# Transposing u on VectorE and through DRAM for the last groups of every batch, with other DMA queues, buffers and load order

## The chip, the cores and the metric

The kernel runs on one core of one Trainium2 chip. The metric is the device time of one execution in microseconds. A core has TensorE (PE, matmuls into PSUM), VectorE (DVE), ScalarE (ACT), GpSimd (POOL) and SyncE (SP), each with an in-order instruction stream of its own. DMAs are issued here from SP's and GpSimd's queues and move their bytes on 16 DMA engines that all queues share.

## The reference

Eight batches of a sequence of 3136 rows by 256 columns. First a filter in the frequency domain along the sequence, then a low-rank mix along the sequence, then a two-layer network along the columns with a residual:

```python
X = np.fft.rfft(x, axis=1)
y = np.fft.irfft(X * F, n=3136, axis=1)            # F: 1569 x 256, complex
u = y + (y.transpose(0, 2, 1) @ U @ V).transpose(0, 2, 1)   # rank 32
out = u + np.maximum(u @ w_ch1, 0.0) @ w_ch2       # 256 -> 1024 -> 256
```

## The kernel before

The Fourier transform of length 3136 is done as 49 x 64. A batch goes through five steps. `f1` (L241; L269 for batches 0 and 1) multiplies the tiles x of the input by the matrix ws, copies the result on ScalarE into a tile asb and stores it to the DRAM tensors ct1 and ct0 from SP. `mid` (L319) loads it back as a2, multiplies by m (matmul pz, L384), by the filter on DVE (uv, L392, L396, L397), transforms back (matmul pe, L345), copies on ScalarE to e and stores to the DRAM tensors ct2 (three parts, L364, from SP). `load_e2` (L412) loads the rows of ct2 into the rows of one tile eb, 256 KB per DMA: for each part one DMA for the half h = 0 (first 32 of 64 slots) and one for h = 1. `rank` (L419) makes the low-rank rows and DVE writes them to eb, too (L438). `s4` (L445) multiplies eb by sv (pu, L456), and DVE and ScalarE copy the result to ut (L463, L461), which holds u transposed: columns of u on partitions, sequence positions along the tile. Its first eight pieces of 16 read the half h = 0 of eb, the others h = 1.

The network then runs over the 8 x 3136 positions in 49 groups of 512. `mm1` (L484) multiplies u by the first weights (phh, L488), ScalarE applies the ReLU (h, L491). `mm2` (L538) multiplies h by the second weights (pc, L544). The residual, adding u itself in its untransposed form, is done in one of two ways:

- Groups before `FIRST_TURNED` (37): `residual` (L527) adds it on PE with eight matmuls of ut against an identity matrix (L536, 128 columns each), and DVE copies the sum from PSUM to och (L556).
- Groups from 37 on, the turned ones: `turn_u` (L499) makes an untransposed copy. DVE transposes ut in blocks of 32 x 32 into a tile tu (L515, two steps), four DMAs store it to DRAM (L520), one DMA loads it back as tur in the right order (L524), and DVE adds it while it evacuates PSUM (L552). All five DMAs are issued from SP.

GpSimd stores each finished group from och (L561, 512 KB) and loads the x tiles (L128).

The order of work is written out by hand. Time is counted in steps, eight to a group: step 8n + t does `mm1` of group n, `mm2` of group n - 1, and then everything in `plan[8n + t]`. The adds or copies to och stand at t = 3 and t = 7, the out store behind t = 7. The steps of a stage run from a = S[b-1] to z = S[b] (48 steps, 56 for the last); in it the groups of batch b - 1 run and batch b is prepared: `mid(b)` from about a - 5 to e, `rank(b)` from e to e + 6, `s4(b)` from e + 8 to z - 2, and `f1(b+1)` from a + 10 to z - 20 (from a + 21 to z - 13 in the first stage). e is z - 17 for b = 1, z - 20 up to b = 5 and z - 22 for b = 6 and 7. The row loads of the three parts stand at e - 5, e - 4 and e + 1, both halves of a part together. The x tiles of batch b + 1 are loaded at a + 1, 5, 9 and 13 (9, 11, 13 and 15 for b = 1). A turned group n has its four steps of `turn_u` at 8n, 8n + 1, 8n + 2 (stores) and 8n + 5 (load). The plan fixes the order in each engine's stream; an engine that need not wait runs ahead of the step at which its instruction stands.

Buffers: the tag x has four of 4 KB per partition, asb four of 4 KB. tu takes its buffers from asb and tur from x.

Of the kernel before, what the change touches and what calls it, by code (L numbers as in the profile page):

```python
# [10 lines left out]
F16 = mybir.dt.float16  # L11
# [3 lines left out]
NB = 8  # L15
# [3 lines left out]
DM = 256  # L19
# [1 line left out]
NH = 1024  # L21
GT = 512
NG = NB * SEQ // GT
FIRST_TURNED = 37

# [53 lines left out]
def kernel(  # L81
# [11 lines left out]
    nc = tc.nc  # L93
# [15 lines left out]
    sb = ctx.enter_context(tc.tile_pool(name="sb", bufs=1))  # L109
    ps = ctx.enter_context(tc.tile_pool(name="ps", bufs=2, space=bass.MemoryType.PSUM))  # L110

    def bank(tag, name, dtype=F32):

        return ps.tile([128, 512 if dtype == F32 else 1024], dtype, tag=tag, bufs=4 if tag == "z" else 2, name=name)

    def dram(t, off, dims):
        return bass.AP(tensor=t, offset=off, ap=[list(d) for d in dims])
# [5 lines left out]
    xt = {}  # L123

    def load_x(b, c):
        t = sb.tile([98, 8 * DM], F16, tag="x", bufs=4, name="x")
        for a, n in ((0, 96), (96, 2)) if b == 0 else ((0, 98),):
            nc.gpsimd.dma_start(t[a:a + n], dram(x.tensor, (b * SEQ + 8 * c + 32 * a) * DM, [[32 * DM, n], [1, 8 * DM]]))  # L128
        xt[b, c] = t
# [10 lines left out]
    for c in range(4):  # L140
        load_x(0, c)
# [64 lines left out]
    tu = eb[0:RANK, 0:12, :].rearrange("p r d -> p (r d)")  # L206
# [34 lines left out]
    def f1(b):  # L241
        for c in range(4):
            t = xt[b, c].rearrange("p (j d) -> p j d", d=DM)
            asb = sb.tile([98, 8, DM], F16, tag="asb", bufs=4, name="asb")
            for half in range(2):
                for i in range(2):
                    pf = bank("z", "pf")
                    for s in range(2):
                        j = 4 * half + 2 * i + s
                        nc.tensor.matmul(pf[0:98, 256 * s:256 * s + 256],  # L250
                                         ws[:, (8 * c + j) * 98:(8 * c + j + 1) * 98], t[:, j, :],
                                         start=(s == 0), stop=True, skip_group_check=True)
                    dst = asb[:, 4 * half + 2 * i:4 * half + 2 * i + 2, :]
                    src = pf[0:98].rearrange("p (j d) -> p j d", d=DM)
                    nc.scalar.copy(dst, src)  # L255
                    if half and i:
                        nc.sync.dma_start(dram(ct1[b], 8 * c * 96 * DM, [[DM, 96], [96 * DM, 8], [1, DM]]), asb[0:96])
                        nc.sync.dma_start(dram(ct0[b], 8 * c * DM, [[32 * DM, 2], [1, 8 * DM]]),
                                          asb[96:98].rearrange("p j d -> p (j d)"))
                    yield  # L260
# [151 lines left out]
    def load_e2(b, part, hs=(0, 1)):  # L412

        n = 12 if (b, part) == (0, 2) else 16
        for h in hs:
            nc.sync.dma_start(eb[32 + part:32 + 4 * n:4, 32 * h:32 * h + 32, :].rearrange("p (q r) d -> p q (r d)", r=8),
                              dram(ct2[b][part], 8 * h * DM, [[NR * DM, n], [16 * DM, 4], [1, 8 * DM]]))
# [61 lines left out]
    groups = [Group(n) for n in range(NG)]  # L479

    def utv(b):
        return ut[b].rearrange("p h q r -> p h (q r)")
# [11 lines left out]


    def turned(gr):
        return gr.n >= FIRST_TURNED

    def turn_u(gr):  # L499

        t = sb.tile([128, 4, 4, 2, 32], F16, tag="asb", bufs=4, name="tu")
        for dh in range(2):
            for b, t0, o, n in gr.seg:
                j, z = o // 32, (o + n) // 32
                while j < z:

                    k = min(z, j + 4 - j % 4) if j % 4 or z - j < 4 else z - z % 4
                    src = utv(b)[:, dh, t0 + 32 * j - o:t0 + 32 * k - o]
                    if k - j < 4:
                        dst = t[:, j % 4:j % 4 + k - j, j // 4, dh, :]  # L510
                        src = src.rearrange("p (c e) -> p c e", e=32)
                    else:
                        dst = t[:, :, j // 4:k // 4, dh, :].rearrange("p c g e -> p g c e")
                        src = src.rearrange("p (g c e) -> p g c e", c=4, e=32)
                    nc.vector.transpose(dst, src)  # L515
                    j = k
            yield
        td = nc.dram_tensor(f"tu_{gr.n}", (128, 4 * DM), F16, kind="Internal")
        for a in range(4):
            nc.sync.dma_start(dram(td, DM * a, [[4 * DM, 32], [128 * DM, 4], [1, DM]]),  # L520
                              t[32 * a:32 * a + 32].rearrange("i c g h e -> i c (g h e)"))
        yield
        gr.tu = sb.tile([128, 4, 4, 2, 32], F16, tag="x", bufs=4, name="tur")
        nc.sync.dma_start(gr.tu.rearrange("p a g h e -> p (a g h e)"), td.ap())  # L524
        yield

    def residual(gr, o, i):  # L527
# [10 lines left out]
    def mm2(gr, t):  # L538
        i, half = t // 2, t % 2
        if t % 4 == 0:  # L540
            gr.pc = bank("o", "pc")
        o = gr.pc[:, 256 * (i % 2):256 * (i % 2) + 256]
        for tt in range(4 * half, 4 * half + 4):
            nc.tensor.matmul(o, gr.h[tt][:, 128 * i:128 * i + 128], w2sb[:, tt, :],  # L544
                             start=(tt == 0), stop=(tt == 7 and turned(gr)), skip_group_check=True)
        if half and not turned(gr):
            residual(gr, o, i)
        if t % 4 == 3:
            if t == 3:
                gr.och = sb.tile([128, 4, DM], F32, tag="och", bufs=2, name="och")  # L550
            if turned(gr):
                nc.vector.tensor_add(gr.och[:, i - 1:i + 1, :].rearrange("p g (h a e) -> p (g h) a e", h=2, a=4),  # L552
                                     gr.pc.rearrange("p (f a e) -> p f a e", f=4, a=4),
                                     gr.tu[:, :, i - 1:i + 1].rearrange("p a g h e -> p (g h) a e"))
            else:
                nc.vector.tensor_copy(gr.och[:, i - 1:i + 1, :], gr.pc.rearrange("p (j d) -> p j d", d=DM))  # L556
            if gr.n == NG - 1:
                nc.sync.dma_start(dram(out.tensor, (gr.n * GT + 128 * (i - 1)) * DM, [[DM, 128], [128 * DM, 2], [1, DM]]),
                                  gr.och[:, i - 1:i + 1, :])
            elif t == 7:  # L560
                nc.gpsimd.dma_start(dram(out.tensor, gr.n * GT * DM, [[DM, 128], [128 * DM, 4], [1, DM]]), gr.och)  # L561
# [3 lines left out]
    plan = [[] for _ in range(8 * NG)]  # L565

    def deal(gen, count, a, z):
        for i in range(count):
            plan[max(0, int(a + i * (z - a) / count))].append(gen)

    def later_x(b, c):
        load_x(b, c)
        yield

    f1s = [f1(b) if b > 1 else f1_turned(b) for b in range(NB)]
    mids = [mid(0, "o")] + [mid(b) for b in range(1, NB)]
    ranks = [rank(b) for b in range(NB)]
    s4s = [s4(b) for b in range(NB)]
    turns = [turn_u(gr) for gr in groups]

    u_hat()
# [4 lines left out]
    for i in range(16):  # L586
# [3 lines left out]
        next(f1s[0])  # L590
    nc.gpsimd.dma_start(sv[32:97], sv_d.rearrange("k (r q) -> k r q", q=NQ))
    load_x(1, 0)
    nc.gpsimd.dma_start(w1sb, moe_w_ch1.rearrange("(h dd) c -> dd h c", h=2))
    spread_filters(2)
# [29 lines left out]
    for _ in s4s[0]:  # L624
        pass

    def loads(b, part):
        load_e2(b, part)
        yield

    for b in range(1, NB):
        a, z = S[b - 1], S[b]
        e = z - (17 if b == 1 else 20 if b < 6 else 22)
        deal(mids[b], 13, a + {1: 8, 2: -3}.get(b, -5), e - 4)
        deal(mids[b], 4, e - 4, e)
        for p, at in enumerate((e - 5, e - 4, e + 1)):
            plan[at].append(loads(b, p))
        deal(ranks[b], 6, e, e + 6)
        deal(s4s[b], 16, e + 8, z - 2)
        if b == 1:  # L640
            deal(f1s[1], 12, 1, 8)
        if b + 1 < NB:
            for c in range(4):
                plan[a + (9 + 2 * c if b == 1 else 1 + 4 * c)].append(later_x(b + 1, c))
            deal(f1s[b + 1], 16, a + (21 if b == 1 else 10), z - (13 if b == 1 else 20))

    for gr in groups:
        if turned(gr):
            for i in range(4):
                plan[8 * gr.n + (0, 1, 2, 5)[i]].append(turns[gr.n])  # L650
    for n, gr in enumerate(groups):
        for t in range(8):
            mm1(gr, t)
# [36 lines left out]
```

## Time and profile before

| | us |
|---|---|
| median of three runs | 518.17 |
| lowest and highest run | 514.89, 519.52 |
| profiled execution | 516.43 |
| its span, first to last instruction | 514.6 |

| engine | busy us | share of span |
|---|---|---|
| PE | 490.5 | 95% |
| DVE | 366.2 | 71% |
| ACT | 377.1 | 73% |
| POOL | 80.6 | 16% |

The rows of costs that matter here:

| line, engine | what | count | mean ns |
|---|---|---|---|
| L488 PE | phh, 128x512 | 672 | 378 |
| L544 PE | pc, 128x256 | 1568 | 272 |
| L536 PE | residual, 128x128 (all forms) | 302 | 219 |
| L392 DVE | uv, 128x1024 | 96 | 1218 |
| L515 DVE | transposes, 128x512 | 22 | 688 |
| L552 DVE | add to och | 24 | 689 |
| L556 DVE | copy to och | 74 | 689 |
| L438 DVE | copies to eb | 32 | 1232 |
| L561 POOL | issue of an out store | 48 | 814 |
| L128 POOL | issue of an x load | 36 | 546 |

The page gives the busy time of each engine, the span in 40 equal slices (a digit is the busy share in tenths; PEclk is the granted clock of PE), and groups of instructions. An answer in order of time gives start, length, engine, line, what is written from what, the count, and in brackets the engine's idle time before it with what ended it. A list of waits gives the total, the number and the longest. PE's durations overlap: a matmul's length in the table is longer than the distance to the next one's start. SP's row loads of the stage that ends at about 289 us were issued at 262 to 265 us (L416, parts 0 and 1) and at 270.52 us (part 2).

### The profile page before, as it was taken

To read this page: it belongs to the slowest core of one execution; us is meant where nothing else is said; L and a number is where in the kernel's file an instruction comes from. 1 tells how busy PE (TensorE), PEld (TensorE's weight loads), DVE (VectorE), ACT (ScalarE), POOL (GpSimd) and SP (SyncE) were. 2 spreads that over 40 slices of the span, in tenths; PEclk is the share of its full clock that TensorE was granted. 3 is DMA by queue.
4 is the path that set the end of the run, shared out by engine and by line. 5 is a ranking of instruction groups with operands and counts; after the bars stand their busy time and mean duration, and the time that the engine had idled before them with its cause. 6 is when DMAs were issued, how large, how long until landed. Compare 5 with 4: busy or idle time off the path is not lost.

```text
span 514.6 us, 11909 instructions
## 1 busy us (share of the span) xinstructions
PE 490.5 (95%) x4754; PEld 349.6 (68%) x4754; DVE 366.2 (71%) x497; ACT 377.1 (73%) x704; POOL 80.6 (16%) x122
## 2 busy tenths in 40 slices
PE   3887899999999999999999999999999998999996
PEld 3645566776767777777767777777677765676665
DVE  5886599579847986679747986679846997853332
ACT  6874778867986689667986689667886676666663
POOL 6662010002001110002001110002001000011110
PEclk9998999999999999999999999999999999999999
DMA  8987926957877286837877286837877136644454
GB/s 187 175 206 174 181 74 172 281 171 176 216 229 251 69 186 190 298 130 177 213 227 254 69 185 202 262 156 184 218 228 240 65 126 206 212 153 149 126 162 163
DMA packets 76016, 94.52 MB, mean 184 GB/s; under 512 B 5795, under 2 KB 58979, under 8 KB 75960
## 3 DMA queue, kind: packets, MB, share of 16 engines
q1 hardware_dynamic: 61256, 52.17, 33.9%
q0 software_dynamic: 14704, 41.58, 31.4%
q8 instruction: 37, 0.61, 0.5%
q14 instruction: 19, 0.16, 0.1%
HBM read 58.35 MB, written 50.92 MB: 212 GB/s over the span
## 4 chain that ended last, share of the span: by engine, by line
PE 81%; DVE 8%; DMA 4%; issue 1%; ACT 1%; SPq 0%; POOL 0%; DVEq 0%; POOLq 0%
PE pc L544 31%; PE phh L488 30%; DVE uv L392 5%; PE pu L456 5%; PE pf L250 4%; PE pe L345 4%; PE pz L384 3%; PE pc L536 3%; DMA w2sb<-in_moe_w_ch_dram 2%; PE ph L423 1%; DVE uv L397 1%; DMA eb<-ct 1%; DVE uv L396 1%; DMA ct<-e 1%; DVE och L556 1%
## 5 line engine op out<-in xcount | busy, mean ns | idle before, releaser
L491 ACT ACTIVATE h<-phh 128x512 f16<-128x512 f32 x392 | 235.9, 603 | 83.2 <-PE phh L488 81.7
L544 PE MATMUL pc<-w2sb,h 128*128 128x256 f16 x1568 | 233.7, 272 | 1.2 <-DMA w2sb<-in_moe_w_ch_dram 1.2
L488 PE MATMUL phh<-ut,w1sb 128*128 128x512 f16 (+7 forms) x896 | 233.3, 352 | 0.4 <-DVE ut L463 0.4
L544 PEld LDWEIGHTS <-h 128*128 128x128 f16 x1568 | 151.7, 97 | 91.8 <-issue 1.5
L392 DVE TENSOR_TENSOR uv<-pz,fab 128x1024 f16<-128x1024 f32 (+1 forms) x104 | 120.6, 1177 | 12.5 <-PE pz L384 10.5
L561 POOL DMA_DIRECT2D out_dram<-och x48 | 39.1, 814 | 402.0 <-DVE och L556 318.8
L488 PEld LDWEIGHTS <-w1sb 128*128 128x128 f16 x896 | 78.9, 97 | 19.8 <-issue 1.5
L556 DVE COPY och<-pc 128x512 f32<-128x512 f32 x74 | 51.0, 689 | 44.4 <-PE pc L536 43.5
L355 ACT CAST e<-pe 128x512 f16<-128x512 f32 x96 | 56.6, 591 | 21.0 <-PE pe L345 20.2
L463 DVE CAST ut<-pu 128x392 f16<-128x392 f32 x92 | 48.5, 557 | 17.9 <-PE pu L456 16.0
L255 ACT CAST asb<-pf 98x512 f16<-98x512 f32 x96 | 57.3, 599 | 0.2
L438 DVE COPY eb<-h 32x4096 f16<-32x4096 f16 x32 | 38.2, 1232 | 14.2 <-ACT h L435 14.2
L552 DVE TENSOR_TENSOR och<-pc,tur 128x512 f32<-128x512 f32 x24 | 16.5, 689 | 39.8 <-PE pc L544 37.3
L345 PE MATMUL pe<-uv,m 128*128 128x512 f16 (+1 forms) x117 | 41.3, 371 | 3.6 <-DVE uv L392 1.5
L456 PE MATMUL pu<-sv,eb 97*128 97x49 f16 x1024 | 40.5, 187 | 3.3 <-DMA eb<-ct 3.1
L456 PEld LDWEIGHTS <-eb 97*128 97x128 f16 x1024 | 37.7, 98 | 4.8 <-DVE eb L438 3.4
L536 PE MATMUL pc<-idn,ut 128*128 128x128 f16 (+1 forms) x302 | 40.8, 219 | 0.0
L384 PE MATMUL pz<-a,m 128*128 128x512 f16 x96 | 36.2, 379 | 1.1 <-DVE a L311 1.0
L250 PE MATMUL pf<-x,ws 98*98 98x256 f16 x192 | 36.6, 273 | 0.0
L396 DVE TENSOR_TENSOR uv<-uv 64x1024 f16<-64x1024 f16 (+1 forms) x49 | 30.9, 630 | 1.7
L536 PEld LDWEIGHTS <-ut 128*128 128x128 f16 (+1 forms) x302 | 28.8, 98 | 3.9 <-issue 0.6
L397 DVE TENSOR_TENSOR uv<-uv 64x1024 f16<-64x1024 f16 (+1 forms) x49 | 30.7, 627 | 0.7
(80 smaller groups left out, 264.9 us busy)
## 6 DMA issues: line engine op xcount, KB each, us to landing
out_dram<-och POOLq DMA_DIRECT2D x48, 512.0 KB, 4.4
ct<-e SPq DMA_DIRECT2D x47, 256.0 KB
eb<-ct SPq DMA_DIRECT2D x46, 256.0 KB
x<-in_x_dram POOLq DMA_DIRECT2D x28, 392.0 KB, 7.8
ct<-asb SPq DMA_DIRECT2D x24, 384.0 KB
a<-ct SPq DMA_DIRECT2D x18, 512.0 KB
tu<-tu SPq DMA_DIRECT2D x48, 64.0 KB
tur<-tu SPq DMA_DIRECT2D x12, 256.0 KB
```

Source lines behind the costliest of these rows:

```text
L250: nc.tensor.matmul(pf[0:98, 256 * s:256 * s + 256], ws[:, (8 * c + j) * 98:(8 * c + j + 1) * 98], t[:, j, :], start=(s == 0), stop=True, s ...
L255: nc.scalar.copy(dst, src)
L345: nc.tensor.matmul(pe[:, 0:n], w, uv[:, f, o:o + n], start=(f == 0), stop=(b > 0 or f == 1))
L355: nc.scalar.copy(t[:, 2 * (i % 2):2 * (i % 2) + 2, :].rearrange("p k d -> p (k d)"), pe)
L384: nc.tensor.matmul(pz, a2m, src[:, k:k + 2, :].rearrange("p k d -> p (k d)"), start=True, stop=True)
L392: nc.vector.tensor_mul(uv[:, :, o:o + n], zin, fin)
L456: nc.tensor.matmul(pu[:, NQ * i:NQ * i + NQ], eb[:, 8 * n + i, d], sv[:, 8 * g + i, :], start=(i == 0), stop=True, skip_group_check=True)
L488: nc.tensor.matmul(ph[:, o:o + n], w1sb[:, dh, 128 * t:128 * t + 128], utv(b)[:, dh, t0:t0 + n], start=(dh == 0), stop=(dh == 1), skip_gro ...
L491: nc.scalar.activation(h, ph, RELU)
L536: nc.tensor.matmul(d, w, idn, start=False, stop=(dh == 1), skip_group_check=True)
L544: nc.tensor.matmul(o, gr.h[tt][:, 128 * i:128 * i + 128], w2sb[:, tt, :], start=(tt == 0), stop=(tt == 7 and turned(gr)), skip_group_check ...
L556: nc.vector.tensor_copy(gr.och[:, i - 1:i + 1, :], gr.pc.rearrange("p (j d) -> p j d", d=DM))
```

## The change

- `FIRST_TURNED` is 38, so group 37 gets its residual on PE again.
- Groups z/8 - 2 and z/8 - 1 of each stage b = 1 to 6 become turned, and z/8 - 3 of stages 2 to 6: groups 4, 5, 9 to 11, 15 to 17, 21 to 23, 27 to 29 and 33 to 35. Their five DMAs are issued from GpSimd's queue; groups from 38 on keep SP's.
- Their four steps of `turn_u` are at z - 36, z - 34, z - 33, z - 29 (group z/8 - 3), e - 3, e - 2, z - 14, z - 10 (z/8 - 2) and e - 1, e, z - 13, z - 8 (z/8 - 1).
- x and asb have three buffers instead of four; tu and tur get two of their own (2 KB each). Three early x tiles lie in asb buffers.
- The row loads go by halves: h = 0 of parts 0, 1 and 2 at e - 5, e - 4 and e + 1, then h = 1 of all three at e + 2.
- The fourth x tile of a batch is loaded at a + 15 instead of a + 13 (a + 25 instead of a + 15 for b = 1).

```diff
-FIRST_TURNED = 37
+FIRST_TURNED = 38
...
     def load_x(b, c):
-        t = sb.tile([98, 8 * DM], F16, tag="x", bufs=4, name="x")
+
+        tag = "asb" if (b, c) in ((0, 3), (1, 0), (1, 1)) else "x"
+        t = sb.tile([98, 8 * DM], F16, tag=tag, bufs=3, name="x")
...
-            asb = sb.tile([98, 8, DM], F16, tag="asb", bufs=4, name="asb")
+            asb = sb.tile([98, 8, DM], F16, tag="asb", bufs=3, name="asb")
...
     def turned(gr):
-        return gr.n >= FIRST_TURNED
+        return gr.n >= FIRST_TURNED or gr.n in turn_at
...
-        t = sb.tile([128, 4, 4, 2, 32], F16, tag="asb", bufs=4, name="tu")
+        t = sb.tile([128, 4, 4, 2, 32], F16, tag="tu", bufs=2, name="tu")
...
+        queue = nc.sync if gr.n >= FIRST_TURNED else nc.gpsimd
         for a in range(4):
-            nc.sync.dma_start(dram(td, DM * a, [[4 * DM, 32], [128 * DM, 4], [1, DM]]),
+            queue.dma_start(dram(td, DM * a, [[4 * DM, 32], [128 * DM, 4], [1, DM]]),
                               t[32 * a:32 * a + 32].rearrange("i c g h e -> i c (g h e)"))
         yield
-        gr.tu = sb.tile([128, 4, 4, 2, 32], F16, tag="x", bufs=4, name="tur")
-        nc.sync.dma_start(gr.tu.rearrange("p a g h e -> p (a g h e)"), td.ap())
+        gr.tu = sb.tile([128, 4, 4, 2, 32], F16, tag="tur", bufs=2, name="tur")
+        queue.dma_start(gr.tu.rearrange("p a g h e -> p (a g h e)"), td.ap())
...
-    def loads(b, part):
-        load_e2(b, part)
+    def loads(b, parts, h):
+        for part in parts:
+            load_e2(b, part, [h])
         yield
+    turn_at = {n: [8 * n + i for i in (0, 1, 2, 5)] for n in range(FIRST_TURNED, NG)}
...
-        for p, at in enumerate((e - 5, e - 4, e + 1)):
-            plan[at].append(loads(b, p))
+        for at, parts, h in ((e - 5, [0], 0), (e - 4, [1], 0), (e + 1, [2], 0), (e + 2, range(3), 1)):
+            plan[at].append(loads(b, parts, h))
+        if b < NB - 1:
+            if b > 1:
+                turn_at[z // 8 - 3] = [z - 36, z - 34, z - 33, z - 29]
+            turn_at[z // 8 - 2] = [e - 3, e - 2, z - 14, z - 10]
+            turn_at[z // 8 - 1] = [e - 1, e, z - 13, z - 8]
...
-                plan[a + (9 + 2 * c if b == 1 else 1 + 4 * c)].append(later_x(b + 1, c))
+                plan[a + (9 + 2 * c + 10 * (c > 2) if b == 1 else 1 + 4 * c + 2 * (c > 2))].append(later_x(b + 1, c))
...
-    for gr in groups:
-        if turned(gr):
-            for i in range(4):
-                plan[8 * gr.n + (0, 1, 2, 5)[i]].append(turns[gr.n])
+    for n, at in turn_at.items():
+        for i in at:
+            plan[i].append(turns[n])
```

## The prediction

> **What bounds the kernel now.** I read the page's slices first, then the list of TensorE's (PE's) waits cut to the steady stretch, then PE in order of time.
>
> ```profile
> PE   3887899999999999999999999999999998999996
> PEclk9998999999999999999999999999999999999999
> ```
>
> PE is near full from the fifth slice on, at full granted clock. But a modelled PE is busy too easily, so the waits decide. Of PE's waits from 115 to 433 us, this is the whole list:
>
> ```profile
> PE pe L345 <- DVE uv L397: 1.3, 1, 1.3
> ```
>
> One wait, 1.33 us, in 318 us: this stretch runs at PE's own pace, so work taken off PE should shorten the span one for one. The chain of waits up to that single wait is DVE's from 410.63 to 432.07 us but for 0.5 us, and the transposes of group 37 stand in it:
>
> ```profile
> 415.16 0.70 DVE uv L392
> 416.50 0.71 DVE tu L515
> 417.21 1.11 DVE uv L392
> 418.32 0.62 DVE tu L515
> 418.94 0.58 DVE och L556
> ```
>
> What the residual costs on PE is read from starts, not from durations, since matmuls overlap:
>
> ```profile
> 251.02 0.59 PE L488 MATMUL phh<-ut,w1sb 128*128 128x512 f16 x2
> 251.46 0.60 PE L544 MATMUL pc<-w2sb,h 128*128 128x256 f16 x4
> 251.89 0.28 PE L536 MATMUL pc<-idn,ut 128*128 128x128 f16 x2
> 252.00 0.38 PE L384 MATMUL pz<-a,m 128*128 128x512 f16 x1
> ```
>
> The two L536 hold PE from 251.89 to 252.00: 0.11 us, or 55 ns each, though the row says 219 ns. DVE, which takes the work over, has its gap here:
>
> ```profile
> 260.32 0.69 DVE L556 COPY och<-pc 128x512 f32<-128x512 f32 x1
> 265.39 0.69 DVE L556 COPY och<-pc 128x512 f32<-128x512 f32 x1 [4.38 <-PE pc L536]
> 268.72 1.22 DVE L438 COPY eb<-h 32x4096 f16<-32x4096 f16 x1 [2.64 <-ACT h L435]
> ```
>
> **PE's share.** Turned groups grow by 2 (batch 0) + 3 x 5 (batches 1 to 5) = 17 and lose group 37: net 16. Each saves 8 L536. 16 x 8 x 55 ns = 7.0 us. All of these groups lie in stretches where PE never waits except at 432 us, so I count all of it.
>
> [...]
>
> **Group 37.** Its transposes stand inside the DVE chain before the 1.33 us wait: 0.69 + 0.69 = 1.38 us (L515, 688 ns mean for 128x512). Without them DVE is ready 1.38 us earlier and the wait closes: -1.3 us. Bounds: 0 (the DVE chain starts later or is filled otherwise) and -1.33. I take -1.3, since the chain has no idle in it. The residual that group 37 gets back (0.44 us) is inside the net 16. Together 8.3 us.
>
> **DVE.** 17 groups x 2 x 0.69 = 23 us more, some 4.1 us in a stage of 57.7. The adds L552 replace copies L556 at the same price (692 and 691 ns median). In the stage 231.3 to 289 DVE is busy 42.6 us, so 46.7 of about 56.4 afterwards. The places: e-3 to e for two groups, 2.8 us, fall into the gaps shown above (4.38 + 2.64 us; 3.67 + 1.91 in the first such stage, 1.99 + 5.33 in the last). The two of group z/8 - 3, at z-36 and z-34, fall where DVE waits 0.73, 1.07, 0.89 and 0.60 us for PE (245 to 258 us); 1.4 of 3.3 us. Cost zero; without that cover at most 1.4 us a stage would be pushed into the uv chain.
>
> **ScalarE** gets nothing. **SP** loses group 37's five DMAs (the first ct<-e store behind them waited until 420.84) and gets the same number of row loads in another order.
>
> **Rows by halves.** PE shows no wait for rows after the start, so the gain is nil. Second halves of parts 0 and 1 move from e-5 and e-4 behind part 2, issued at 270.52 in the stage I follow (e there is 266.15). They are first read at 280.88 (the ninth pair of pu). Ahead of the last half lie 1 MB of rows, a 512 KB store and, as GpSimd runs ahead, 512 KB of tu: 2.1 MB at some 300 GB/s (this trace moved 312 in 262 to 268, 277 in 271 to 279) is 7 us, so about 278, plus up to 2 us for landing. Hidden by 1 to 3 us; taken as 0. Bounds: 0 (PE waits for no row now, so none can come better), and 2 us in each of six stages if they land 2 us after their reading is due.
>
> **GpSimd's queue.** Before, it had out stores and x loads alone (80.6 us busy in all). Per turned group: four stores and one load at some 0.55 us of issue each (the x load's 546 ns mean is the nearest row), 47 us in all on a queue that mostly waits. The queue is in order, but nothing on it waits for z-14: after the out store of step z-17 (271.15 + 1.13 = 272.28) the stores of groups z/8 - 2 and z/8 - 1 go at once, as DVE was done with them before. What stands behind: the load of group z/8 - 2 needs its stores landed, the out store of z-9 stands behind that load (nobody needs its buffer for another 8 steps), then the load of group z/8 - 1. The critical one is the first: it must land before the add at z-5, 283.76 here. Eight stores back to back end near 276.7; the first group's fourth starts at 273.9. A small GpSimd DMA lands in 3.9 to 4.8 us (eb<-e, 32 KB): 278.3. Then the load, 256 KB: nearest rows are out_dram at 3.2 to 6.0 us and x at 5.7 to 9.1 in the steady part; I take 5: 283.3. That is just in time. DVE waiting there holds up L463, and PE has four pu/pz banks, enough from 283.76 to 286.25: 2.5 us of lateness is free. Taken: 0.3 us over the kernel.
>
> **x, three buffers.** The load of c=3 moves behind the out store of step a+15. Out ends at 135.7, 193.3, 252.8, 309.1 and 367.5 us; c=3 is first read at 144.16, 201.93, 259.95, 317.73 and 376.16. That leaves 8.4, 8.6, 7.1, 8.6 and 8.7 us; in batch 0's stage, behind the out store that ends at 87.3, 7.9 until 95.14. An x load alone behind an out store landed in 6.0 to 6.2 us at quieter steps; the second of a pair in 7.9 to 9.1. Out stores at a+15 took 3.8 to 5.4 against about 3.5 at a+7, so I add 1: 7.2, a loss of 0.1 us, rounded up to 0.5 for the six stages. Bounds: 0, and at 9.1 us 0.7 + 0.5 + 2.0 + 0.5 + 0.4 + 1.2 = 5.3 us. The asb tiles, three now, are refilled some 12 us after the store that frees them (248.16 and 260): nothing. The start loses a wait on x (1,0) that no one stands behind on the chain: nothing.
>
> **Sum.** 7.0 + 1.3 - 0.3 - 0.5 = 7.5 us. Against the profiled execution, 516.43 (span 514.6 and 1.83 around it): 508.9. That execution lies 1.7 us under the median of 518.17 (514.89 to 519.52), so in terms of the median **510.7 us**, 1.45% less.
>
> **Rivals.**
> 1. *x late.* c=3 lands 8.7 to 9.1 us after its issue instead of 7.2, and PE waits in L250: by the margins above 2.9 to 5.3 us in all. For it: the 7.1 us margin, and SP's traffic is heavier there (46% of the DMA engines in 250 to 262 from its queue). Against: four margins of six exceed 8. Of 8.0 us 2.7 to 5.1 are left: 513.1 to 515.5, within 1%. Chance 0.18.
> 2. *tur late, slower.* The load on GpSimd's queue lands so late before z-5 that DVE blocks, L463 stops and PE runs out of banks. Price: lateness less 2.5 us, in six stages. It eats the gain from 3.9 us late (6 x 1.4 = 8.3), and makes the kernel slower by 1% from 4.7 us late: 6 x 2.25 = 13.5 us, less 8.3, is 5.2. For it: the margin is about nothing, GpSimd's issue beside L438 took 1.13 us against 0.75, and the stores stand right beside three more L438; x at the start landed as late as 11.4. Against: the load is 256 KB where x is 392. Chance 0.20: 0.08 around 516 to 520, 0.12 at 523 to 526. [...]
> 3. *More than 55 ns.* If the weight load of 98 ns in front of each L536 were exposed, 128 x 98 = 12.5 us would go: 504. PE's starts speak against it. Chance 0.05.
>
> **Numbers.** Forecast 0.57 (gain 6 to 8.3: 509.9 to 512.2). A measurement of this kernel can tell about 1%, 5.2 us. Faster by over 1%: 0.57 + 0.05 = 0.62. Within: 0.18 + 0.08 = 0.26. Slower: 0.12. The range goes from the fastest run less 7.9 (507) to no gain (518); outside lie rival 3 and most of the slow half of 2, about 0.17. The forecast's own range is 508 to 513.
>
> **What would show it.** L536 at 174 instead of 302; L515 on DVE at 60 instead of 28 (28 + 34 - 2); stages of about 56.4 us instead of 57.7; the 1.33 us wait at L345 gone. Rival 1: PE L250 waiting for DMA x. Rival 2: DVE L552 waiting for DMA tur by more than 2.5 us, and PE L456 or L384 waiting for DVE. Rows late: PE L456 waiting for DMA eb<-ct after 100 us. I am wrong if none of these shows and the stages keep their length: then PE was not the bound.

## The result and the profile after

| | before | after |
|---|---|---|
| median | 515.04 us | 529.17 us |
| lowest and highest | 514.31, 519.52 | 526.40, 533.04 |
| profiled execution, span | 516.43, 514.6 | 526.40, 524.6 |
| mean granted clock | 0.995 | 0.985 |

The ratio of the times is 1.0259, with a 95% interval of 1.0222 to 1.0296: the kernel is 2.6% slower. The forecast was 1.45% faster. Medians here and below are over all executions; the ratios leave out the one slow execution that four of the experiments had, over 1.5% above the fastest of its kernel.

PE's work shrank as predicted: the residual matmuls (L540 now) fell from 302 to 174. But PE's waits, from 115 to 440 us, were one of 1.33 us, and are now these (total, number, longest):

```profile
PE pu L458 <- DVE ut L465: 5.4, 5, 1.4
PE pz L386 <- DVE uv L394: 3.1, 4, 0.8
PE pe L347 <- DVE uv L399: 0.8, 1, 0.8
PE pu L458 <- issue: 0.5, 1, 0.5
PE pf L252 <- DMA x<-in_x_dram: 0.5, 1, 0.5
PE pu L458 <- DMA eb<-ct: 0.5, 1, 0.5
```

The first two are new in kind: PE waits for DVE to empty the PSUM buffers of pu and pz. Why DVE is late is told by the chain that ended last, here in stage 2 (start, length, what):

```profile
152.70 0.70 DVE och L560
153.68 1.13 POOL out_dram L565
154.82 2.82 POOL tu L524 x3
157.64 6.04 DMA tu<-tu
163.80 0.51 issue
164.32 4.50 DMA tur<-tu
168.94 0.69 DVE och L556
```

A chain that was PE's is now GpSimd's queue: out store, stores of group z/8 - 2, their landing, the load, its landing, and only then the add at z - 5. GpSimd issues no store before the out store of step z - 17, since its queue is in order. DVE's own stream shows the price:

```profile
165.25 0.57 DVE L465 CAST ut<-pu 128x392 f16<-128x392 f32 x1 [0.24 <-PE pu L458]
168.94 0.69 DVE L556 TENSOR_TENSOR och<-pc,tur 128x512 f32<-128x512 f32 x1 [3.12 <-DMA tur<-tu]
169.54 0.55 DVE L465 CAST ut<-pu 128x392 f16<-128x392 f32 x1
```

It sits for 3.12 us in front of an add, with the casts of ut behind it that PE's banks wait for. PE at the same time:

```profile
168.26 0.60 PE L548 MATMUL pc<-w2sb,h 128*128 128x256 f16 x4
170.15 0.37 PE L458 MATMUL pu<-sv,eb 97*128 97x49 f16 x8 [1.29 <-DVE ut L465]
171.28 0.59 PE L386 MATMUL pz<-a,m 128*128 128x512 f16 x1 [0.76 <-DVE uv L394]
171.66 1.06 PE L490 MATMUL phh<-ut,w1sb 128*128 128x512 f16 x2
172.52 1.06 PE L548 MATMUL pc<-w2sb,h 128*128 128x256 f16 x4
173.37 1.06 PE L490 MATMUL phh<-ut,w1sb 128*128 128x512 f16 x2
```

The two idle times are 2.05 us. After them two L490 take 0.86 us from start to start (171.66 to 172.52), where they took 0.44 before: PE runs at half its clock. The windows (us, busy time and count of each engine, granted clock, DMA share, GB/s) agree:

```profile
168.00:170.00 2.00, 0.86 (x6) 0.48 (x5) 1.06 (x2) 0.60 (x1) 0.00 (x0) 1.00 0.50 162
170.00:172.00 2.00, 1.09 (x10) 0.53 (x10) 2.00 (x4) 0.49 (x1) 0.00 (x0) 0.76 0.01 2
172.00:174.00 2.00, 2.00 (x8) 1.03 (x7) 1.97 (x3) 0.60 (x1) 0.00 (x0) 0.50 0.00 0
174.00:176.00 2.00, 2.00 (x18) 1.38 (x16) 1.73 (x4) 0.90 (x2) 0.03 (x1) 0.88 0.00 0
```

DVE waits for tur in front of the add at z - 5 by 3.12, 2.40, 3.24, 3.28 and 3.39 us in stages 2 to 6, and by 5.85 us at 456 us, in stage 7, the last (b = 7, up to step 336). That last one is the add of group 39, 13 steps before the end of its stage, and the DMAs there are SP's:

```profile
456.41 0.69 DVE L556 TENSOR_TENSOR och<-pc,tur 128x512 f32<-128x512 f32 x1 [5.85 <-DMA tur<-tu]
```

In stage 1 DVE does not wait for tur.

**Where the time went.** The start cost nothing: the changed kernel begins step 48, with the residual of one group saved, at 113.94 us (first L548), the kernel before at 115.16 us (first L544), although its half-clock stretch at the start lasts 6.83 us and that of the kernel before 3.41. With a span that grew by 10.0 us, it then loses 11.2 us up to the end. PE idle, from 115 to 505 us: 13.8 us instead of 1.6, so +12.2. Half clock: two stretches of 3.41 us after 115 us at a granted clock of 0.50, each losing half, +3.4. Residual: -7.0. That is +8.6; 2.6 us are in none of these terms. Some 2.0 of them, by an estimate, are the way in which idle time is counted: four L544 last 0.60 us in the trace before, but the next matmul starts 0.43 us after their start (251.46 and 251.89 us), so each stall is some 0.17 us longer than the idle time listed, and there are twelve more of them than before. The rest is open. The profiled execution is the fastest of six; the others lie up to 6.6 us above it.

### The profile page after: what moved, and what is told of

It is laid out like the page before. It is cut to its first block, busy times and chain, and to the rows that moved or that the text cites. A ratio compares the mean times of both kernels' runs of the same rounds, so it can differ in the third digit from the quotient of the medians.

```text
span 524.6 us, 11757 instructions
## 1 busy us (share of the span) xinstructions
PE 490.3 (93%) x4626; PEld 344.8 (66%) x4626; DVE 384.1 (73%) x529; ACT 376.3 (72%) x704; POOL 134.8 (26%) x207
## 4 chain that ended last, share of the span: by engine, by line
PE 54%; DMA 17%; DVE 10%; issue 9%; POOL 4%; ACT 1%; SPq 0%; DVEq 0%; POOLq 0%
PE phh L490 20%; PE pc L548 20%; DMA tu<-tu 6%; DMA tur<-tu 5%; DVE uv L394 5%; PE pf L252 3%; DMA x<-in_x_dram 3%; PE pe L347 3%; POOL tu L524 2%; PE pz L386 2%; PE pu L458 2%; DMA ct<-e 2%; POOL out_dram L565 2%; DVE och L556 1%; PE pc L540 1%
## 5 line engine op out<-in xcount | busy, mean ns | idle before, releaser
L490 PE MATMUL phh<-ut,w1sb 128*128 128x512 f16 (+7 forms) x896 | 235.8, 355 | 0.4 <-DVE ut L465 0.2
L548 PE MATMUL pc<-w2sb,h 128*128 128x256 f16 x1568 | 234.8, 273 | 0.5 <-DMA w2sb<-in_moe_w_ch_dram 0.5
L548 PEld LDWEIGHTS <-h 128*128 128x128 f16 x1568 | 152.3, 98 | 92.7 <-issue 3.0
L490 PEld LDWEIGHTS <-w1sb 128*128 128x128 f16 x896 | 80.1, 98 | 24.7 <-issue 6.4
L556 DVE TENSOR_TENSOR och<-pc,tur 128x512 f32<-128x512 f32 x56 | 38.6, 688 | 62.5 <-PE pc L548 39.4
L458 PEld LDWEIGHTS <-eb 97*128 97x128 f16 x1024 | 39.5, 99 | 16.0 <-issue 11.5
L524 POOL DMA_DIRECT2D tu<-tu x68 | 44.9, 668 | 6.9 <-DMA out_dram<-och 6.7
L560 DVE COPY och<-pc 128x512 f32<-128x512 f32 x42 | 28.7, 684 | 22.9 <-PE pc L540 22.4
L517 DVE STREAM_TRANSPOSE tu<-ut 128x512 f16<-128x512 f16 (+2 forms) x60 | 36.9, 652 | 0.4
```

The lines of the kernel that those rows point to most:

```text
L458: nc.tensor.matmul(pu[:, NQ * i:NQ * i + NQ], eb[:, 8 * n + i, d], sv[:, 8 * g + i, :], start=(i == 0), stop=True, skip_group_check=True)
L490: nc.tensor.matmul(ph[:, o:o + n], w1sb[:, dh, 128 * t:128 * t + 128], utv(b)[:, dh, t0:t0 + n], start=(dh == 0), stop=(dh == 1), skip_gro ...
L524: queue.dma_start(dram(td, DM * a, [[4 * DM, 32], [128 * DM, 4], [1, DM]]), t[32 * a:32 * a + 32].rearrange("i c g h e -> i c (g h e)"))
```

## The experiments

Times are medians, ratios are to the kernel before on the same chip. All edits are to the changed kernel.

**Without the second of the three groups.** Is it the late tur of z/8 - 2?

```diff
-            turn_at[z // 8 - 2] = [e - 3, e - 2, z - 14, z - 10]
```

> Groups z/8 - 2 of the six stages are not turned; the other eleven new ones are. Theory (the late tur of these groups on GpSimd's queue makes DVE and then PE wait, five times about 3 us on DVE): no DVE wait for tur in stages 1 to 6; the gain of ten groups is 10 x 0.44 = 4.4 us; the stall of the last stage (4.6 us, rows by halves) stays: 514 to 518 us. Rival (the extra DMA traffic or the other edits cost the time): 523 to 528 us, PE waits as in the changed kernel.

Measured: 509.38 us, ratio 0.9883 (0.9854 to 0.9911). DVE never waits for tur, and this is all that PE waits for from 115 to 440 us:

```profile
PE pu L458 <- issue: 1.4, 1, 1.4
```

The wait is in front of pu, and the profile shows nothing that it was for. Six groups fewer turned bring some 19 us. The theory held and the rival did not, but the time lies 4.6 us below the range expected, as the last stage's stall is gone, too. Why it is gone is not shown: the order of that stage's DMAs is the same.

**Rows whole.** Both halves of a part together again, at e - 5, e - 4 and e + 1.

```diff
-        for at, parts, h in ((e - 5, [0], 0), (e - 4, [1], 0), (e + 1, [2], 0), (e + 2, range(3), 1)):
+        for at, parts, h in ((e - 5, [0], 0), (e - 4, [1], 0), (e + 1, [2], 0)):
...
-            load_e2(b, part, [h])
+            load_e2(b, part)
```

> Row loads as before, both halves of a part together, all else as changed. Theory (the halves cost time only in the last stage, where the tur load of group 39 stands behind four row loads in SP's queue): the 5.85 us DVE wait for tur near 456 us shrinks to 1 to 2 us, 4 to 5 us come back: 523 to 526 us, the five waits for tur on GpSimd's queue stay at about 3 us. Rival (the halves protect the rows, which GpSimd's stores now crowd): PE waits for rows in every stage, 532 us or more.

Measured: 528.58 us, ratio 1.0266 (1.0213 to 1.032). Half of the theory failed. The last stage's wait for tur shrank from 5.85 to 1.59 us, as expected, but no time came back, as the rival's effect took its place. Of the five waits for tur on GpSimd's queue, which were to stay, two are left (1.64 and 2.83 us), and PE waits for the rows instead:

```profile
PE pu L458 <- DMA eb<-ct: 15.3, 8, 3.9
```

With GpSimd's stores among them, whole rows come late: 15.3 us of PE over the kernel, where the changed kernel has 3.0, 2.5 of them at the start. The halves protect the rows that the other edit crowds.

**No new turned group.** Buffers, x loads, row halves and group 37 as changed.

```diff
-        if b < NB - 1:
+        if False:
```

> No group of batches 0 to 5 is turned; groups from 38 on are. Buffers, row halves, x loads as changed. Theory: against the kernel before plus 0.4 us (residual of group 37), minus up to 1.3 us (its transposes), plus the last stage's stall of 4 to 5 us: 517 to 520 us. Rival (the buffers of three or the later x loads cost as much as the turned groups): 522 us or more. If the row halves cost nothing by themselves: 514 to 515 us.

Measured: 514.65 us, ratio 0.9983 (0.9958 to 1.0008). From 115 to 436 us PE waits for nothing at all: the wait of 1.33 us is gone with group 37's transposes, and neither three buffers nor the later x cost anything. The time is the one expected if the row halves cost nothing by themselves. The stall of the last stage is small here, too: one wait of 2.4 us on DVE, none on PE.

**Early stores.** Only the order on GpSimd's queue.

```diff
-            turn_at[z // 8 - 2] = [e - 3, e - 2, z - 14, z - 10]
+            turn_at[z // 8 - 2] = [e - 3, e - 2, e - 1, z - 16]
```

> Only the order on GpSimd's queue: the stores of group z/8 - 2 stand at e - 1 and its load at z - 16, ahead of the stores of group z/8 - 1. Theory: tur lands before z - 5, the five DVE waits of about 3 us go, with them some 8 to 10 us: 518 to 521 us, the last stage's stall stays. Rival (the DMA engines are too full there, whatever the order): the stores meet the rows of parts 0 and 1, PE waits for rows or x instead, 526 us or more.

Measured: 515.40 us, ratio 0.9972 (0.9941 to 1.0003); the profiled execution 512.02. The same 17 groups and the same bytes, and some 14 us less; the theory held, with more time back than expected. GpSimd's stream in stage 2:

```profile
146.92 2.18 POOL L524 DMA_DIRECT2D tu<-tu  x4
154.24 1.13 POOL L565 DMA_DIRECT2D out_dram<-och  x1 [5.13 <-DVE och L560]
155.36 1.15 POOL L528 DMA_DIRECT2D tur<-tu  x1
```

The load goes out at 155.36 instead of 164.32, and DVE waits for tur only in the last stage (4.48 us). The DMA engines are as full as in the changed kernel: 0.93 of the time in 153 to 167 us, against 0.92 there in 154 to 168 (0.67 before the change, 155 to 169). So it is not the fullness as such, but a dependent pair, store and load, that was started too late in it.

**Early stores, last stage's halves later.**

```diff
-(e + 2, range(3), 1)
+(e + (2 if b < NB - 1 else 4), range(3), 1)
```

> As the run with early stores, and in the last stage with row loads the second halves stand at e + 4, behind the tur load of group 39. Theory (that stage's wait was the tur load behind four row loads on SP's queue): the 4.5 us DVE wait for tur near 444 us goes and with it about 2 to 4 us of PE: 511 to 513 us, if the rows wait of 1.8 us stays. Rival (that stall has another cause, or executions of this order differ because rows and stores meet): no change, 515 us.

Measured: 513.74 us, ratio 0.9963 (0.994 to 0.9987). PE's wait of 1.7 us in the last stage is gone, and the next tur is late by 2.2 us on DVE without PE noticing. The intervals of the two runs overlap, so the gain is not shown by the times. From 115 us on PE still waited 2.0 us for rows, and 2.7 us in front of pu for nothing that the profile shows.

**The second group turned in the middle of the stage**, with stage 1 and the last stage's halves as above.

```diff
-                turn_at[z // 8 - 3] = [z - 36, z - 34, z - 33, z - 29]
+                turn_at[z // 8 - 3] = [z - 36, z - 34, z - 33, z - 28]
-            turn_at[z // 8 - 2] = [e - 3, e - 2, z - 14, z - 10]
+            turn_at[z // 8 - 2] = [e - 3, e - 2, e - 1, z - 16] if b == 1 else [z - 32, z - 30, z - 29, z - 24]
```

> All 17 groups turned, but group z/8 - 2 of stages 2 to 6 is transposed at z - 32 and z - 30, stored at z - 29 and loaded at z - 24, before the rows come; stage 1 with early stores; second row halves of the last stage at e + 4. Theory (only the place of these DMAs among the rows was at fault, the transposes fit into DVE's slack): no wait for tur or rows, the whole 7.0 us and more: 506 to 509 us. Rival (DVE is too full in the middle of a stage, or x is now late behind more stores): PE waits for DVE uv or DMA x, 512 us or more.

Measured: 510.65 us, ratio 0.9914 (0.9886 to 0.9941). No wait for tur is left, and DVE has room for the transposes there: PE has no wait for uv after 115 us. PE waits 2.2 us for rows in that stretch. I put that down to the load at z - 24, which now meets the rows of parts 0 and 1; the run below with its load behind the rows does not bear this out. The time is 1.7 us above the range of the theory.

**The DMAs on SP's queue.**

```diff
-        queue = nc.sync if gr.n >= FIRST_TURNED else nc.gpsimd
+        queue = nc.sync
```

> As changed, but all turned groups' DMAs on SP's queue. If it was GpSimd's slower issue and landing (6.4 us for a store of 64 KB) that made tur late: tur comes in time, 515 to 521 us. If it is the place among the rows: SP issues them behind the row halves and ahead of the loads of a, tur is as late or later, 525 us or more.

Measured: 532.18 us, ratio 1.0308 (1.026 to 1.0355). SP's queue, at the same steps, is no better: the time is the one that the rival gave, by another path than it named. On SP tur is late on DVE in three places only (5.4 us), but PE is late there itself, so whether GpSimd's slower issue (medians in the changed kernel's trace: 0.55 us for a store of tu and 0.56 for a load, against 0.46 and 0.34 on SP) had a part in the late tur is not shown. The loads of a for the next batch stand behind eight stores and two loads on SP's queue, and PE waits for them:

```profile
PE pz L386 <- DMA a<-ct: 13.1, 5, 3.6
```

**Whole rows without the second group.** The first two edits together.

> Group z/8 - 2 not turned and rows whole, as before the change. Theory: with half as much on GpSimd's queue in the rows' time the rows are late by less than in the run with whole rows and all groups (PE waits 15 us): PE waits for rows 0 to 5 us, 510 to 515 us. Rival (halves matter only with both groups): the same as with halves, 509 us.

Measured: 522.53 us, ratio 1.0152 (1.0116 to 1.0188); PE waits 8.4 us for rows from 115 to 436 us. The theory had the mechanism and too small a price (0 to 5 us of waiting, 510 to 515 us), and two of the stalls were followed by 3.4 us of half clock each (mean granted clock 0.99 from 115 to 436 us). Against the run without the second group, which has halves, the halves are worth 13 to 14 us, with just one group's stores among the rows.

**The second group in the middle, its load behind the rows.** As the mid-stage run, but not in stage 1, and:

```diff
-                turn_at[z // 8 - 2] = [e - 3, e - 2, z - 14, z - 10]
+                turn_at[z // 8 - 2] = [z - 32, z - 30, z - 29, z - 12]
```

> As the run with group z/8 - 2 turned in the middle of the stage, but its tur load stands at z - 12, behind the stores of group z/8 - 1, so that it no longer meets the rows of parts 0 and 1; in stage 1 that group is not turned. Theory (what is left there, 0.3 to 2.0 us of PE waiting for rows per stage, comes from DMAs of turned groups in the rows' time): PE waits for rows 0 to 1 us in all, 507 to 509 us. Rival (the rows are late because of the traffic of the out store and of group z/8 - 1's stores): no change, 510 to 511 us.

Measured: 509.14 us, ratio 0.9887 (0.9853 to 0.9922), the lowest median of all, no different from the run without the second group. Rows still cost 3.0 us of PE from 115 to 505 us, one wait of 1.6 and one of 1.4 us, where the run before this change of place had 2.2. The theory, 0 to 1 us, failed: that the load's place at z - 24 makes the rows late is not shown, and what does is open.

**Group 37 turned again**, without the second group.

```diff
-FIRST_TURNED = 38
+FIRST_TURNED = 37
```

> Group z/8 - 2 not turned, and group 37 turned again from SP's queue. By the prediction's term the DVE chain before the end of mid(7) gets 1.38 us longer and PE waits there again: +1.3 - 0.44 = 0.9 us slower than without it, 510 to 511 us. Rival (DVE's chain has slack by now): 0.4 us faster, 509 us.

Measured: 511.25 us, ratio 0.9917 (0.9891 to 0.9944), the expected direction against 509.38 us and 0.9883, but the intervals overlap, so the times do not show it. The trace shows the wait. DVE's chain catches PE again:

```profile
425.08 0.39 PE L347 MATMUL pe<-uv,m 128*128 128x512 f16 x1 [1.52 <-DVE uv L399]
```

## Why the prediction was wrong

**The step that failed** is "GpSimd's queue", whose sum put the load's landing at 283.3 us against an add at 283.76 and took 0.3 us for it. The chain was drawn right, in its order and place. Three of its terms were too small, two of them taken from rows measured in a quieter time:

- Issue of the three stores ahead of the fourth: 3 x 0.55 = 1.65 us; measured 2.82 in stage 2, as two of the eight stores take 1.15 us each beside DVE's copies to eb. (All eight take 5.54 us, where the sum had 4.4, but the last has been issued before the first group's stores have landed.)
- Landing of a store: 4.4 us, from a 32 KB DMA at the start; measured 6.4 us median over GpSimd's 68 stores, 6.04 in the chain above.
- From that landing to the issue of the load: nothing; measured 0.64 us, of which the chain lists 0.51 as issue.

The landing of the load itself (5 us taken) came at 4.50. From the end of the out store's issue to the landing of the load the sum had 11.0 us; the chain took 14.0, and DVE was ready for the add after 11.0. So the load is late by 3.0 us, and DVE waited 3.12. The slack of PE behind a late DVE, 2.5 us from counting banks, was too large as well: in stage 2 PE lost 2.05 of the 3.12 us, so the slack was 1.1 us; it was 1.1 in stages 3 to 5, too, and 2.7 in stage 6.

What was named as the slower rival, with a chance of 0.20, is what happened, in the mechanism and in five of its six stages; its 523 to 526 us lie 3 to 6 us under the 529.17 measured, and further in proportion, since they stand on a median of 518.17 us before the change, where the six runs give 515.04.

**A term that was missing** is the clock. A wait of PE was priced at its own length; two of the stalls were also followed by 3.4 us at a granted clock of 0.50, which cost 1.7 us each. In the run on SP's queue there were four such stretches between 100 and 420 us (mean granted clock 0.98 from 115 to 436 us).

**SP's queue in the last stage** was read too quickly: "the same number of row loads in another order" is true, but the order puts the second halves of parts 0 and 1 ahead of the tur load of group 39 in an in-order queue. Four row loads go out ahead of it:

```profile
445.81 2.44 SPq L418 DMA_DIRECT2D eb<-ct  x4
448.55 0.35 SPq L528 DMA_DIRECT2D tur<-tu  x1
```

Issued at 448.55, that load landed 7.7 us later (4.4 us in the kernel before), and DVE waited 5.85 us. In the six traces that have this order and group 39's load behind it (the changed kernel, no second group with and without group 37, none new, early stores, SP's queue) the add of group 39 starts 5.3 to 7.9 us after the load's issue; in the kernel before and the two runs with whole rows it is 4.4 to 4.8 us. So the order delays the load, but DVE's wait ranges from 5.85 us to none under the same order; what sets its size is open, and the times do not separate it.

**Rows by halves**: no gain by itself, as argued, but 13 to 14 us next to one group's stores and as a whole what kept the rows in time. I had priced what the halves cost, and not what whole rows would have cost beside the new traffic. The prediction's 2 us for landing were an estimate; in the kernel before, the out store issued at 115.70 us landed 3.2 us later, 1.5 us more than its 512 KB take at 300 GB/s.

**Right:** the 55 ns per residual matmul. From no new group (514.65) to eleven (509.38) are 5.3 us, 0.48 a group, where 8 x 55 ns is 0.44. The traces show it more closely: in the run with group 37 turned again PE waits for nothing between steps 96 and 288 (170.13 to 398.18 us), and that stretch is 3.55 us shorter than in the kernel before (173.38 to 404.98), for eight turned groups: 0.44 a group, 55 ns a matmul. Group 37: its wait goes without its transposes and comes back with them. DVE's cover: even in the middle of a stage the transposes bring PE no wait. x: two waits of 0.3 and 0.5 us, 0.9 in all, of 0.5 forecast. And that PE was the bound: work taken from it shortens the kernel wherever nothing new is late.

**Open:** the profiled execution with early stores lies 3.4 us under its median, and what the others lost is in no trace. Nor was it tried what the last 3 us of row waits come from, or which of the DMAs in the rows' time makes whole rows late.

## What to carry to other kernels

When work is moved off a saturated engine by a round trip through DRAM, cost the round trip as a chain at its place: what the issuing queue does before it, and landing times measured while the DMA engines are as full as they will be there (6.4 us for a store of tu among the rows, where 4.4 had been taken from the start). With as little slack as here, 1.1 us behind a late DVE in four of five stages, a late transfer is paid for at once, so place a dependent store and load far from the transfers that are already on time, and far ahead of their use. Then check who stands behind the new DMAs in each in-order queue.

## What the runs showed of the hardware

In the changed kernel's trace PE's granted clock is 0.50 in three stretches before the last matmuls: 6.83 us from 44.76 us, 3.41 us from 171.06 us and 3.41 us from 457.77 us. The kernel before has one, 3.41 us from 45.22 us. The three starts lie 126.30 and 286.71 us apart, 37 and 84 times such a length (3.413 us by their sum).

Stalls of nearly the same length were not followed by the same clock. PE's idle times of 1.29 us (up to 170.15 us) and 0.76 us (up to 171.28) came with half clock from 171.06 us, and one of 2.79 us (up to 457.62) with half clock from 457.77. Those of 1.40 us (up to 290.32 us) and 0.77 us, and of 1.45 us (up to 349.28 us) and 0.76 us, did not: the granted clock is 1.00 from 286 to 296 and from 346 to 356 us. So a stall of some 2 us cost its own length in two stages and 1.7 us more in one; what decides between them is not shown.
